# Expert 2's rows gathered inside expert 0's further tiles, and weights issued ahead of the turning of tiles 4 and 5

## The chip, the cores and the metric

The kernel runs on one core of a Trainium2 chip. A core has five engines with a queue each: TensorE (PE, matmuls), VectorE (DVE), ScalarE (ACT), GpSimd (POOL) and SyncE (SP), which here only issues transfers. Each queue works in order; the engines wait for each other through semaphores. Transfers issued by SP and POOL run on the core's 16 DMA engines. The metric is the device time of one execution in microseconds (us); lower is better.

## What is computed

A banded attention (8 batches, 8 heads, 576 positions, 64 per head) and behind it a mixture of 8 experts, top 1, on its 4608 rows of 512 numbers. Cut to what matters here:

```
logits = x @ w_gate;  e_idx = argmax(logits)
for e in range(8):
    mask = e_idx == e
    h = relu(x[mask] @ w1[e])                       # 512 -> 1024
    out[mask] = gate_w[mask] * eom[mask, e] * (h @ w2[e])   # 1024 -> 512
```

x is the attention's output. All is float32 at the interface. Which rows belong to an expert is known only when the gate of the last rows has been computed.

## The kernel before

The first 185 us or so are the attention, the gate and the ranking that gives every token a place in its expert's list (`src` holds the row numbers). Then the experts follow one after another, and the change lies there.

Each expert has up to SLOTS = 6 tiles of 128 rows. Tiles 0 to 3 (BASE = 4) always run; tiles 4 and 5 run as far as the expert has rows, through a `tc.Switch` with five bodies at the end of each expert's pass (L1346), the first of which (`nothing`) runs no further tile. Expert 0 is special: its first three tiles (HEAD = 3) run while the last rows are still being ranked (`head`, with `during_first` and `during_second`), and its next two in `two_more(0, HEAD, xx, next_x)`. Behind these stands a Switch for rare cases (L1284), whose second body (`repair`) computes expert 0's first tiles again where a late row displaced an early one.

A matrix product in float32 is made of three products of parts: each operand is split into a rounded part and a remainder. The names that the profile shows:

- `wraw`: four staging buffers of 512 KB in which `load_w(e, kind)` puts a quarter each of an expert's first (kind 0) or second matrix, four DMAs on SP (L114). `split_w` makes the two parts: ACT rounds (L132), DVE subtracts (L136). The subtract frees the staging buffer for the next load.
- `xg[0]` to `xg[3]` (the profile calls them sd) and `xg[4]`, `xg[5]` (xg): tiles of rows. `gather_rows(e, ...)` fetches an expert's rows into them with one indirect DMA for each tile, on POOL (L152).
- `turn_rows(e, ...)` brings a tile's rows into the order in which a 32 by 32 transpose on DVE completes the turn: SP writes the tile to the DRAM buffer `xq` in blocks (L170) and reads it back (L175), and the read waits for the landing of the write.
- `prep4`: the transpose on DVE (L190), the rounding on ACT (L197), the subtract on DVE (L198). Tiles 0 to 3 become `X` (sc in the profile), tiles 4 and 5 `xx` (xxh, xxl).
- `base_h` and `products1` (L210): the products with the first matrix, 12 matmuls for each of the NF = 8 blocks of 128 columns of h, into the accumulators `ph` (tpx). `relu` (L216 on ACT, L217 on DVE) makes the two parts of h.
- `gemm2` (L946): the products with the second matrix; `finish` scales (L953, L955), and `scatter` (L959, POOL) writes rows to the output.

The order on every engine is written out by hand: the whole section stands in `tc.manual_schedule` for all five engines, so each queue holds its instructions in the order of the program. In the pass of expert e the first products' blocks 2 to 7 carry the splits of its own second matrix (blocks 2 to 5), the gathers and the turning; the second products carry the splits of the next expert's first matrix and, after each, the `prep4` of one of its tiles, then `prep4` of tiles 4 and 5, then the gathers for expert e + 2. Blocks 0 and 1 of the next expert (`start(e + 1)`, and `fill` or a body's own calls) are queued on the TensorE around the Switch.

So for SP the order in the pass of an expert e above 1 is: turning of expert e + 1's four tiles (at the third block), turning of tiles 4 and 5 of expert e (at the sixth block), the four loads of expert e + 1's first matrix, the four of its second. For e = 1 the gathers of expert 2 stand at the third block behind those of tiles 4 and 5, and the turning of expert 2's rows stands at the sixth block, behind that of tiles 4 and 5 and ahead of the loads.

Of the kernel before, what the change touches and what calls it, by code (L numbers as in the profile page):

```python
# [31 lines left out]
BASE = 4  # L32
# [4 lines left out]
HEAD = 3  # L37
# [13 lines left out]
def kernel(  # L51
# [58 lines left out]
    def load_w(e, kind):  # L110
        src = (w1, w2)[kind]
        for c in range(4):
            t = stage.tile([P, 1024], F32, name="wraw")
            nc.sync.dma_start(out=t, in_=src[e, :, 1024 * c : 1024 * c + 1024])  # L114
            raws[e, kind, c] = t
# [22 lines left out]
    def split_w(e, kind, c, sub=nc.vector):  # L138
        split_hi(e, kind, c)
        split_lo(e, kind, c, sub)  # L140

    def part_of(w, a, o, n):
        return w[a][o // 1024][:, o % 1024 : o % 1024 + n]
# [3 lines left out]
    def where(e, j):  # L147
        s = e * SLOTS + j
        return idx[:, s : s + 1], scl[:, s : s + 1]

    def gather(j, at, rows=N):
        nc.gpsimd.indirect_dma_start(  # L152
            out=xg[j],
            out_offset=None,
            in_=xs[0:rows],
            in_offset=bass.IndirectOffsetOnAxis(ap=at.bitcast(U32), axis=0),
            bounds_check=rows - 1,
            oob_is_err=False,
        )

    def gather_rows(e, *js):
        if e < E:
            for j in js:
                gather(j, src[:, e * SLOTS + j : e * SLOTS + j + 1])

    def turn_rows(e, *js):
        if e < E:
            rows = {j: xq[P * (e * SLOTS + j) : P * (e * SLOTS + j) + P] for j in js}
            for j in js:
                nc.sync.dma_start(  # L170
                    out=rows[j].rearrange("(q s) (a f) -> (s a) q f", q=4, a=4),
                    in_=xg[j].rearrange("p (q f) -> p q f", q=4),
                )
            for j in js:
                nc.sync.dma_start(out=xg[j], in_=rows[j])  # L175

    def bank(ps, name):
        return ps.tile([P, 512], F32, name=name)

    def prep(j, xh, xl, k, tp):  # L180
        for c in range(NC):
            nc.tensor.transpose(out=tp[:, P * c : P * c + P], in_=xg[j][:, P * c : P * c + P], identity=idn)
        r = slice(P * k, P * k + P)
        tv = tp.rearrange("p (c t) -> p c t", c=NC)
        nc.scalar.copy(out=xh[:, :, r], in_=tv)
        nc.vector.tensor_tensor(out=xl[:, :, r], in0=tv, in1=xh[:, :, r], op=ALU.subtract)

    def prep4(j, xh, xl, k):
        t = xg[j]
        nc.vector.transpose(out=t, in_=t)  # L190
        r = slice(P * k, P * k + P)

        def view(ap):
            return ap.rearrange("p c (a s) -> p c a s", a=4)

        tv = t.rearrange("p (a c s) -> p c a s", a=4, c=NC)
        nc.scalar.copy(out=view(xh[:, :, r]), in_=tv)  # L197
        nc.vector.tensor_tensor(out=view(xl[:, :, r]), in0=tv, in1=view(xh[:, :, r]), op=ALU.subtract)  # L198
# [5 lines left out]
    def products1(e, fc, xh, xl, m, ph, chunks=range(NC), parts=(0, 1)):  # L204
        w = W[e, 0]
        for c in chunks:
            o = F * c + P * fc
            for a, x in ((0, xh), (0, xl), (1, xh)):
                if a in parts:
                    nc.tensor.matmul(  # L210
                        ph[:, 0:m], lhsT=part_of(w, a, o, P), rhs=x[:, c, 0:m],
                        start=c == 0 and x is xh and a == 0, stop=c == NC - 1 and a == 1,
                    )
# [8 lines left out]
    def base_h(e, fc, X, m, hs=None, ph=None):  # L222
        hh, hl = hs or hb[fc]
        return gemm1(e, fc, *X, m, ph or bank(ps_h, "ph"), hh[:, 0:m], hl[:, 0:m])
# [750 lines left out]
    def pair_x():  # L975
        return [mp.tile([P, NC, 2 * P], F32R, name=n) for n in ("xxh", "xxl")]
# [5 lines left out]
    def start(e):  # L982
        base_h(e, 0, X, BASE * P)
        return bank(ps_h, "ph")

    def go_on(ph):
        return [hb[0], relu(BASE * P, ph, *hb[1])]
# [57 lines left out]
    def choose(e):  # L1045
        flag[e] = nc.values_load(cnt[0:1, 2 * E + 3 + e : 2 * E + 4 + e], min_val=0, max_val=len(PATHS))
        flag[e, "hint"] = tc.switch_hint({t: flag[e] for t in HINTED}, len(PATHS) + 1, f"paths{e}")
# [77 lines left out]
    def two_more(e, j, xx, between=None):  # L1125
        h = []
        for fc in range(NF):
            if fc % 2 == 0:
                eh = ep.tile([P, 512], F32R, name=f"eh{fc // 2}")
                el = ep.tile([P, 512], F32R, name=f"el{fc // 2}")  # L1130
            r = slice(2 * P * (fc % 2), 2 * P * (fc % 2) + 2 * P)
            h.append(gemm1(e, fc, *xx, 2 * P, bank(ps_x, "tpx"), eh[:, r], el[:, r]))
        if between:
            between()
        for k in range(2):
            y = bank(ps_y, "y")
            for fc in range(NF):
                gemm2(e, fc, h[fc], k, y)
            finish(k == 0, *where(e, j + k), y)
# [117 lines left out]
    def next_x():  # L1257
        for j in range(BASE):
            prep4(j, *X, j)

    two_more(0, HEAD, xx, next_x)
    ph = start(1)
# [2 lines left out]
    def repair():  # L1265
        with tc.If(flag[0] > (HEAD + 2) * P):
            late = pair_x()
            prep(SLOTS - 1, *late, 0, bank(ps_x, "tpx"))
            extra(0, SLOTS - 1, late, 1, 0)
        with tc.If(flag["redo"] > 0):  # L1270
            places = [where(0, j) for j in range(HEAD)]
            for j in range(HEAD):
                gather(j, places[j][0])
            for j in range(HEAD):
                prep(j, *X, j, bank(ps_x, "tpx"))
            head(X, places, bank(ps_z, "z"), alone=True)
            gather_rows(1, *range(HEAD))
            turn_rows(1, *range(HEAD))
            for j in range(HEAD):
                prep4(j, *X, j)  # L1280
            base_h(1, 0, X, BASE * P)
            products1(1, 1, *X, BASE * P, ph)

    for n in tc.Switch(flag["rare"], 2, flag["rare", "hint"]):  # L1284
        products1(1, 1, *X, BASE * P, ph, (1, 2, 3))
# [3 lines left out]
    for e in range(1, E):  # L1289
        xx = pair_x()  # L1290
        h = go_on(ph)
        for fc in range(2, NF):
            h.append(base_h(e, fc, X, BASE * P, ph=bank(ps_x, "tpx") if fc % 4 > 1 else None))
            if fc == 2:
                gather_rows(e, 4, 5)
                if e > 1:
                    turn_rows(e + 1, *range(BASE))
                else:
                    gather_rows(2, *range(BASE))
            if fc < 6:  # L1300
                split_w(e, 1, fc - 2)
                if fc == 5:
                    turn_rows(e, 4, 5)
                    if e == 1:
                        turn_rows(2, *range(BASE))
                    if e + 1 < E:
                        load_w(e + 1, 0)
        choose(e)
        ys = [bank(ps_y, "y"), bank(ps_z, "z"), bank(ps_y, "y"), bank(ps_z, "z")]
        for fc in range(NF):  # L1310
            for j in range(BASE):
                gemm2(e, fc, h[fc], j, ys[j])
            if e + 1 < E and fc < 4:
                split_w(e + 1, 0, fc)
                if fc == 3:
                    load_w(e + 1, 1)
                prep4(fc, *X, fc)
            if fc in (4, 5):
                prep4(fc, *xx, fc - 4)
            if fc == 5:  # L1320
                if e > 2:
                    nc.gpsimd.drain()
                gather_rows(e + 2, *range(BASE))
        for j in range(BASE):
            finish(j % 2, *where(e, j), ys[j])
        fill = ()
        if e + 1 < E:
            ph = start(e + 1)
            fill = [lambda cs=cs: products1(e + 1, 1, *X, BASE * P, ph, cs) for cs in ((0,), (1,), (2, 3))]

        def nothing():
            for f in fill:
                f()

        def two():
            nothing()
            two_more(e, BASE, xx)

        bodies = [
            nothing,  # L1340
            lambda: extra(e, BASE, xx, 0, 1, fill),
            lambda: extra(e, BASE, xx, 1, 0, fill),
            lambda: extra(e, BASE, xx, 1, 1, fill),
            two,
        ]
        for n in tc.Switch(flag[e], len(bodies), flag[e, "hint"]):  # L1346
            bodies[n]()
# [165 lines left out]
```

## Time and profile before

| what | us |
|---|---|
| median of 3 runs (613.67 to 616.11) | 614.93 |
| the profiled execution | 612.23 |
| its span, first to last instruction | 610.5 |
| TensorE busy in the span | 579.5 (95%) |
| DVE, ACT, POOL busy | 351.8, 259.7, 219.3 |
| mean granted TensorE clock | 0.989 of full |

In the profile "idle before" and the brackets at the end of a line name the time an engine stood still ahead of an instruction and what let it go; "issue" means that it waited for nothing that the profile shows. PEld is the TensorE's load of weights into the array; a "q" behind an engine's name (SPq, POOLq, PEldq) marks work of its queue that is not counted as busy, such as issuing a DMA, a branch or a wait. "In order of time" is the view that lists the instructions of a stretch with their start and length; times count from the start of the span. In this run expert 1 takes its Switch's first body, as do experts 3 and 5.

### The profile page before, as it was taken

To read this page: it belongs to the slowest core of one execution; us is meant where nothing else is said; L and a number is where in the kernel's file an instruction comes from. 1 tells how busy PE (TensorE), PEld (TensorE's weight loads), DVE (VectorE), ACT (ScalarE), POOL (GpSimd) and SP (SyncE) were. 2 spreads that over 40 slices of the span, in tenths; PEclk is the share of its full clock that TensorE was granted. 3 is DMA by queue.
4 is the path that set the end of the run, shared out by engine and by line. 5 is a ranking of instruction groups with operands and counts; after the bars stand their busy time and mean duration, and the time that the engine had idled before them with its cause. 6 is when DMAs were issued, how large, how long until landed. Compare 5 with 4: busy or idle time off the path is not lost. (4 is left out here: it accounts for less than half of the span.)

```text
span 610.5 us, 13435 instructions
## 1 busy us (share of the span) xinstructions
PE 579.5 (95%) x5102; PEld 467.7 (77%) x5103; DVE 351.8 (58%) x621; ACT 259.7 (43%) x418; POOL 219.3 (36%) x364
## 2 busy tenths in 40 slices
PE   7799999998999999979999998999999999999995
PEld 6677777776787988868888887887588778758884
DVE  5888988899699335175561563563256456435020
ACT  4579665678443224144341442442244244233020
POOL 7788778788117214024131113013121310211021
PEclk8999999999999999989999999999999999999998
DMA  7998989896525914867756467747145764303021
GB/s 206 344 337 272 320 295 298 238 333 184 201 80 166 300 53 146 278 201 224 246 189 201 161 216 251 231 157 225 43 148 198 247 229 139 114 11 100 3 72 37
DMA packets 67509, 117.42 MB, mean 192 GB/s; under 512 B 7776, under 2 KB 44128, under 8 KB 65776
## 3 DMA queue, kind: packets, MB, share of 16 engines
q1 hardware_dynamic: 59904, 95.45, 47.9%
q0 software_dynamic: 6944, 19.15, 10.2%
q8 instruction: 67, 1.10, 0.8%
q14 instruction: 130, 1.06, 0.6%
q10 hardware_dynamic: 464, 0.66, 0.3%
HBM read 88.48 MB, written 30.28 MB: 195 GB/s over the span
## 5 line engine op out<-in xcount | busy, mean ns | idle before, releaser
L959 POOL DMA_INDIRECT out_dram<-yt,idx x39 | 38.6, 991 | 136.8 <-ACT yt L955 79.9
L152 POOL DMA_INDIRECT sd<-xs,src x28 | 29.4, 1048 | 122.7 <-DVE sc L198 120.5
L210 PE MATMUL ph<-sc,w 128*128 128x512 f32 x240 | 60.5, 405 | 3.2 <-ACT sc L197 3.2
L136 DVE TENSOR_TENSOR w<-wraw,w 128x1024 fp32r<-128x1024 f32 x40 | 49.2, 1233 | 18.1 <-ACT w L132 18.1
L210 PE MATMUL tpx<-sc,w 128*128 128x512 f32 x240 | 56.3, 390 | 2.9 <-issue 1.9
L210 PEld LDWEIGHTS ph<-sc,w 128*128 128x128 f32 x240 | 46.4, 195 | 15.4 <-ACT sc L197 3.7
L210 PEld LDWEIGHTS tpx<-sc,w 128*128 128x128 f32 x240 | 44.8, 188 | 13.2 <-issue 2.8
L946 PE MATMUL y<-w,h 128*128 128x512 f32 x190 | 53.9, 391 | 1.0 <-DVE w L136 1.0
L386 POOL TENSOR_TENSOR half<-half 128x128 f32<-128x128 f32 (+3 forms) x136 | 45.3, 333 | 10.7
L132 ACT CAST w<-wraw 128x1024 fp32r<-128x1024 f32 x40 | 41.6, 1044 | 10.4 <-DMA wraw<-in_w_dram 9.9
L946 PE MATMUL z<-w,h 128*128 128x512 f32 x152 | 43.5, 389 | 0.0
L946 PEld LDWEIGHTS y<-w,h 128*128 128x128 f32 x190 | 35.4, 188 | 8.6 <-issue 1.4
L197 ACT CAST sc<-sd 128x512 fp32r<-128x512 f32 x28 | 17.4, 621 | 53.1 <-DVE sd L190 53.1
L380 POOL TENSOR_TENSOR half<-pt 128x256 f32<-128x256 f32 x34 | 30.0, 882 | 11.3 <-ACT pt L375 9.9
L217 DVE SCALAR_TENSOR_TENSOR h<-tpx,h 128x512 fp32r<-128x512 f32 x28 | 19.4, 691 | 24.8 <-ACT h L216 24.7
L955 ACT ACTIVATE yt<-y,scl 128x512 f32<-128x512 f32 x19 | 12.9, 688 | 47.8 <-PE y L946 47.6
L946 PEld LDWEIGHTS z<-w,h 128*128 128x128 f32 x152 | 28.5, 188 | 5.9
L216 ACT ACTIVATE h<-tpx 128x512 fp32r<-128x512 f32 x28 | 16.8, 599 | 38.0 <-PE tpx L210 35.6
L198 DVE TENSOR_TENSOR sc<-sd,sc 128x512 fp32r<-128x512 f32 x28 | 19.4, 692 | 20.5 <-ACT sc L197 20.5
L375 ACT ACTIVATE pt<-pt 128x512 f32<-128x512 f32 x36 | 22.7, 632 | 18.8 <-DVE pt L365 14.6
L152 POOL DMA_INDIRECT xg<-xs,src x14 | 17.2, 1231 | 36.2 <-DMA sd<-xq 9.6
L361 DVE TENSOR_REDUCE mx<-sp 128x8 f32<-128x512 f32 x36 | 24.7, 685 | 8.5 <-PE sp L346 8.3
(296 smaller groups left out, 1393.9 us busy)
## 6 DMA issues: line engine op xcount, KB each, us to landing
wraw<-in_w_dram SPq DMA_DIRECT2D x64, 512.0 KB, 4.0
xq<-sd SPq DMA_DIRECT2D x28, 256.0 KB, 4.8
sd<-xq SPq DMA_DIRECT2D x28, 256.0 KB, 5.3
xs<-wraw SPq DMA_DIRECT2D x29, 128.0 KB, 5.7
xq<-xg SPq DMA_DIRECT2D x14, 256.0 KB, 2.3
xg<-xq SPq DMA_DIRECT2D x14, 256.0 KB, 2.7
sd<-in_qT_dram SPq DMA_DIRECT2D x6, 576.0 KB, 5.5
sa<-in_kT_dram SPq DMA_DIRECT2D x6, 576.0 KB, 6.8
```

The lines of the kernel that those rows point to most:

```text
L132: nc.scalar.copy(out=W[e, kind][0][c], in_=raws[e, kind, c])
L136: sub.tensor_tensor(out=w[1][c], in0=raws.pop((e, kind, c)), in1=w[0][c], op=ALU.subtract)
L152: nc.gpsimd.indirect_dma_start(out=xg[j], out_offset=None, in_=xs[0:rows], in_offset=bass.IndirectOffsetOnAxis(ap=at.bitcast(U32), axis=0) ...
L198: nc.vector.tensor_tensor(out=view(xl[:, :, r]), in0=tv, in1=view(xh[:, :, r]), op=ALU.subtract)
L210: nc.tensor.matmul(ph[:, 0:m], lhsT=part_of(w, a, o, P), rhs=x[:, c, 0:m], start=c == 0 and x is xh and a == 0, stop=c == NC - 1 and a == 1,)
L217: nc.vector.scalar_tensor_tensor(out=hl, in0=ph[:, 0:m], scalar=0.0, in1=hh, op0=ALU.max, op1=ALU.subtract)
L361: nc.vector.tensor_reduce(out=mx, in_=sp.rearrange("p (h k) -> p h k", h=H), axis=AX.X, op=ALU.max)
L375: nc.scalar.activation(out=pt, in_=pt, func=AF.Exp, scale=1.0 / 8.0)
L380: nc.gpsimd.tensor_tensor(out=half.rearrange("p (h c) k -> p h c k", c=2), in0=pv[:, :, :, 0:32], in1=pv[:, :, :, 32:64], op=ALU.add)
L386: nc.gpsimd.tensor_tensor(out=dst, in0=half[:, :, 0:n], in1=half[:, :, n : 2 * n], op=ALU.add)
L946: nc.tensor.matmul(y, lhsT=l[:, r], rhs=part_of(w, a, DM * fc, DM), start=fc == 0 and n == 0, stop=fc == NF - 1 and n == 2)
L959: put = nc.gpsimd.indirect_dma_start(out=out, out_offset=bass.IndirectOffsetOnAxis(ap=at.bitcast(U32), axis=0), in_=yt, in_offset=None, bo ...
```

## The change

The gathers of expert 2's four tiles, and of tile 4 of expert 1, move from the third block of expert 1 into `next_x`, which `two_more` calls for expert 0 between the first and the second products, right behind the `prep4` of expert 1's tiles. `repair` fetches again what it overwrites. The turning of expert 2's rows moves to the third block of expert 1, where the other experts have theirs. In all experts the loads of the next expert's first matrix are issued ahead of the turning of tiles 4 and 5, on SP.

```
@@ -1257,6 +1257,8 @@
     def next_x():
         for j in range(BASE):
             prep4(j, *X, j)
+        gather_rows(2, *range(BASE))
+        gather_rows(1, 4)
...
@@ -1280,6 +1282,8 @@
             products1(1, 1, *X, BASE * P, ph)
+        gather_rows(2, *range(HEAD))
+        gather_rows(1, 4)
...
@@ -1292,19 +1296,14 @@
             if fc == 2:
-                gather_rows(e, 4, 5)
-                if e > 1:
-                    turn_rows(e + 1, *range(BASE))
-                else:
-                    gather_rows(2, *range(BASE))
+                gather_rows(e, *((4, 5) if e > 1 else (5,)))
+                turn_rows(e + 1, *range(BASE))
             if fc < 6:
                 split_w(e, 1, fc - 2)
                 if fc == 5:
-                    turn_rows(e, 4, 5)
-                    if e == 1:
-                        turn_rows(2, *range(BASE))
                     if e + 1 < E:
                         load_w(e + 1, 0)
+                    turn_rows(e, 4, 5)
```

## Prediction

> **What bounds the kernel now.** I read the page first (the busy shares, the slices and the costliest groups), then the table of waits of the TensorE, then the order in time of each engine around the one long wait in the stretch that the change touches, and last the TensorE's branches.
>
> ```profile
> PE 579.5 (95%) x5102; PEld 467.7 (77%) x5103; DVE 351.8 (58%) x621; ACT 259.7 (43%) x418; POOL 219.3 (36%) x364
> ```
>
> The TensorE is busy for 579.5 of 610.5 us, so this change can only be worth the TensorE's idle time that it takes away, and the time at a low clock behind it. The table of waits of the TensorE from 190 us on (engine and line, who let it go, sum, times, longest) says how much there is:
>
> ```profile
> PE tpx L210 <- issue: 3.4, 2, 1.9
> PE ph L210 <- ACT sc L197: 3.2, 1, 3.2
> ```
>
> One wait of 3.2 us stands out: block 0 of expert 2 waits for the rows of expert 2 (sc) to be split. In order of time on the TensorE, with the same pair of blocks of a later expert for comparison, and the granted clock of the slow stretch (columns: stretch, length, PE, PEld, DVE, ACT, POOL busy, clock, DMA share, GB/s):
>
> ```profile
> 266.03 0.84 PE L946 MATMUL z<-sb,h 128*128 128x512 f32 x3
> 270.12 8.52 PE L210 MATMUL ph<-sc,w 128*128 128x512 f32 x24 [3.24 <-ACT sc L197]
> ...
> 372.27 5.60 PE L210 MATMUL ph<-sc,w 128*128 128x512 f32 x24
> 270.10:278.40 8.30, 8.28 (x24) 6.30 (x25) 5.33 (x8) 3.01 (x5) 3.86 (x4) 0.66 0.70 224
> ```
>
> The gap is 3.24 us, and the 24 matmuls behind it take 8.52 us at a mean clock of 0.66 where the same 24 take 5.60 us elsewhere. The bubble costs 3.24 + 2.92 = 6.16 us. Its cause stands in the order of time of ACT, DVE and SP in expert 1:
>
> ```profile
> 255.73 1.05 ACT L132 CAST w<-wraw 128x1024 fp32r<-128x1024 f32 x1 [9.93 <-DMA wraw<-in_w_dram]
> 270.10 0.69 DVE L198 TENSOR_TENSOR sc<-sd,sc 128x512 fp32r<-128x512 f32 x1 [0.69 <-ACT sc L197]
> 234.97 2.06 SPq L170 DMA_DIRECT2D xq<-xg  x2
> ...
> 240.59 4.91 SPq L170 DMA_DIRECT2D xq<-sd  x4
> ...
> 248.66 13.32 SPq L114 DMA_DIRECT2D wraw<-in_w_dram  x6
> ```
>
> SP is a queue in order. It issues the turning of tiles 4 and 5 (xg), then that of expert 2's rows (sd), and only at 248.66 the weights of expert 2. ACT waits 9.93 us for the first of these, and the chain split, turn, split behind it ends with the subtract at 270.10, 3.4 us after the TensorE is through with expert 1 (266.03 + 0.68 = 266.71).
>
> **The change part by part.** *Four gathers of expert 2 and one of tile 4, on POOL inside expert 0's further tiles.* Each sd is free when its last subtract is done, and POOL is idle there but for the scatters of expert 0:
>
> ```profile
> 220.22 0.69 DVE L198 TENSOR_TENSOR sc<-sd,sc 128x512 fp32r<-128x512 f32 x1 [0.69 <-ACT sc L197]
> 221.85 0.98 POOL L959 DMA_INDIRECT out_dram<-yt,idx  x1 [17.33 <-DVE yt L953]
> 232.65 1.04 POOL L152 DMA_INDIRECT xg<-xs,src  x1 [7.67 <-ACT h L216]
> L1284 POOLq INC_SWDGE_SEM  x1: 520/520/520, 228.1 to 228.1; - x1
> 214.93 0.32 SPq L175 DMA_DIRECT2D sd<-xq  x1
> ```
>
> The fourth gather is free at 220.91 and tile 4's follows; at 1.0 us and 0.3 us between them they end at 223.5, so the scatters go out up to 2 us later than now. Nobody computes on a scatter; what is queued behind them is POOL's own passage of the rare branch, where it lets its outstanding transfers land and bumps their semaphore at 228.1. I put that near 230 after the change, and tile 5's gather stays near 233. DVE and ACT get no instruction more. Cost on the path: nothing, covered by POOL's idle 17.33 us.
>
> *Turning of expert 2's rows at the third block.* SP can take it as soon as POOL has passed the branch, about 230; it took 8.1 us before (240.59 to 248.66), so it ends near 238. Early bound: 219, if only the landings hold it (SP leaves its last turn at 214.93); late bound: 234.97, SP's first issue now, and then 243.
>
> *Weights of expert 2 ahead of the turning of tiles 4 and 5.* A load needs its staging buffer, which the splits of expert 1's second matrix free on DVE; and it needs its time to land:
>
> ```profile
> 241.33 1.23 DVE L136 TENSOR_TENSOR sb<-wraw,sb 128x1024 fp32r<-128x1024 f32 x1 [0.24 <-ACT sb L132]
> DMA to landing us min/median/max: 3.5/3.9/10.6
> ```
>
> The four go out between 238 and 242.6 instead of 248.66 to 250. The first lands near 242, at worst near 248.6; ACT has been free for it since 255.73 − 9.93 = 245.80. The 9.93 us of waiting goes (at worst 2.8 of it stays), and the whole chain moves up by as much: its last subtract starts at 260.17 and ends 5.85 us before 266.71. That margin swallows even the worst landing. The gap goes, and the low clock with it: −6.16 us.
>
> *Turning of tiles 4 and 5 behind the weights.* In expert 1 SP reaches it at about 243 (the last load at 242.6). The two pairs took from 234.97 to 240.59, so the rows are there by about 252 with a landing; they are used at 270.70 − 9.93 = 260.77. In the later experts the turning waits for the fourth split as well:
>
> ```profile
> 270.70 0.70 DVE L190 STREAM_TRANSPOSE xg<-xg 128x512 f32<-128x512 f32 x1
> 290.35 1.81 SPq L170 DMA_DIRECT2D xq<-xg  x2
> 291.18 1.22 DVE L136 TENSOR_TENSOR w<-wraw,w 128x1024 fp32r<-128x1024 f32 x1 [0.24 <-ACT w L132]
> 298.68 1.05 ACT L132 CAST sa<-wraw 128x1024 fp32r<-128x1024 f32 x1 [3.02 <-DMA wraw<-in_w_dram]
> 313.70 0.70 DVE L190 STREAM_TRANSPOSE xg<-xg 128x512 f32<-128x512 f32 x1
> ```
>
> In expert 2 it moves from 290.35 to about 292.8, and its rows are wanted at 313.70, or 3.02 us sooner since that wait of ACT goes too: some 10 us to spare. These 3.02 us buy nothing, for the TensorE does not wait there. Experts 3 to 6 have the same order with no wait of either kind: nothing.
>
> *What is late next.* Behind block 0 and 1 of the next expert stands a branch of several ways, and the TensorE takes it while it works off 24 queued matmuls (5.45 us, from 1.4 us after the first). The branch's duration in ns and its start (the rare branch, expert 1's, expert 3's), the DMA share of the stretches of the last two, the TensorE's two gaps by issue, behind the branches of experts 3 and 5, and SP's last load and first turning around the branches of experts 3 and 1:
>
> ```profile
> L1509 PEldq COMPARE_BRANCH  x1: 4175/4175/4175, 224.2 to 224.2; - x1
> L1509 PEldq COMPARE_BRANCH  x1: 3327/3327/3327, 273.2 to 273.2; - x1
> L1509 PEldq COMPARE_BRANCH  x1: 5972/5972/5972, 373.7 to 373.7; - x1
> 272.00:277.00 5.00, 5.00 (x16) 3.90 (x15) 3.73 (x6) 2.45 (x5) 1.82 (x3) 0.63 0.56 161
> 373.00:381.00 8.00, 6.08 (x27) 4.76 (x26) 0.92 (x2) 0.60 (x1) 2.84 (x4) 1.00 0.94 310
> 379.79 1.38 PE L210 MATMUL tpx<-sc,w 128*128 128x512 f32 x5 [1.92 <-issue]
> 489.49 1.63 PE L210 MATMUL tpx<-sc,sa 128*128 128x512 f32 x6 [1.51 <-issue]
> 369.73 2.31 SPq L170 DMA_DIRECT2D xq<-sd  x4
> 268.82 0.33 SPq L114 DMA_DIRECT2D wraw<-in_w_dram  x1
> 274.19 1.38 SPq L170 DMA_DIRECT2D xq<-sd  x2
> ```
>
> With the DMA engines at 0.94 the branch took 5.97 us, 1.9 us more than the queued matmuls cover; at 0.56 it took 3.33 us. In expert 3 SP turned the next rows at 369.73, 2.5 us before block 0 at 372.27. In expert 1 now it does so at 274.19, 4.1 us after block 0 at 270.12, so its branch was quick. With the chain 9.93 us sooner, the last load leaves at about 258.9 and the turning, 5.37 us behind it as now, at 264.3 or sooner: 2.4 us before block 0 at 266.71. Expert 1 gets the timing of expert 3, and I take the mean of the two such gaps, 1.92 and 1.51: +1.72 us. The ends are 0 (the quick branch) and 1.92. No clock is lost with it: around the 1.92 us gap the clock stayed at 1.00 (the stretch from 373 to 381).
>
> Two other branches come nearer to traffic. The rare one at 224.2 ends 0.1 us after its cover; the five gathers and later scatters add to a stretch in which few transfers run. The nearest row is itself: 0, with −0.1 (3.33 us) and +1.8 us (5.97 us) as ends. Expert 2's turning comes 3.02 us earlier, to about its block 0; in expert 4 it stood there too (next fence) and no gap followed: 0, at most +2.
>
> ```profile
> 417.96 2.88 PE L210 MATMUL ph<-sc,w 128*128 128x512 f32 x12
> 418.14 2.66 SPq L170 DMA_DIRECT2D xq<-sd  x4
> ```
>
> The sum: −3.24 − 2.92 + 1.72 = −4.44 us. The profiled execution took 612.23 us (span 610.5, 1.7 outside it), so it becomes 607.8; its runs' median is 2.7 us higher, 614.93, and becomes 610.5 us.
>
> **The rivals.** *The next branch stays quick.* If SP's turning of expert 2 starts only at 234.97, the chain moves up by 5 us rather than 9.93, the rows of expert 3 are turned after the branch has its code, as now, and the gap is still gone. 614.93 − 6.16 = 608.8. For it: two quick branches of 3.33 and 4.18 us; against it: the two with a turning just ahead of the block were followed by the gaps.
>
> *One more branch is hit.* If SP is not held by POOL's passage, it turns expert 2's rows from about 219 on, and the rare branch at 224.2 runs into that traffic: 5.97 us, +1.8 us, 612.3. The same price, about, if it is expert 2's branch. For it: the gathers land by then; against it: POOL holds its semaphores until 228.1 now. The Trainium skill, "Runtime: NRT & Kernel Launch", Instruction fetch mechanics, speaks for this rival: a taken branch out of the loaded window waits for a DMA to bring the code. The trace agrees, with 5.97 us at a DMA share of 0.94 against 3.33 us at 0.56.
>
> *It does not do what it says.* The turning of expert 2's rows, still ahead of the weights on SP, begins, for a wait that I do not see, no sooner than at 240.59; the weights then go out at 248.66 and all stays: 614.9. Against it: the two pairs of xg no longer stand before it.
>
> *The low clock has another cause.* Then the 3.24 us of gap go and the 2.92 us stay: 614.93 − 3.24 + 1.72 = 613.4. Against it: of the two pairs of blocks above only the one behind the long gap ran at 0.66. The Trainium skill, "TensorE: Matmul & The Clock Gate", Part 1, would give this result, for it halves the clock after an idle window of about 3.4 us, which a gap of 3.24 us need not fill. The trace differs, with 0.66 right behind that gap.
>
> *Slower.* The rows of tile 5 come late: their transpose on DVE stands ahead of expert 1's result scaling and of block 0's relu of expert 2. Lateness up to 266.71 is covered by the 5.85 us of margin; 6.16 − 1.72 = 4.4 us more eat the gain, so from a landing at about 271 on (if the TensorE has to follow at once) the kernel loses. At 275 it would be 618.9. Against it: about 252 by the rows, 19 us earlier.
>
> **How the numbers follow.** Forecast 0.52, quick branch 0.20, one more branch 0.18, no effect 0.04, clock 0.02, slower 0.04. 0.5% is about what a measurement of this kernel can tell from no change; 3.07 us of gain is reached by the forecast (4.4; I leave 0.02 of it below) and by the quick branch: faster 0.70. Same: 0.02 + 0.18 + 0.04 + 0.02 = 0.26. Slower: 0.04. The forecast's own range is 609.3 to 611.7 (the runs now lie 1.2 us to each side). With the quick branch at 608.8 less part of that spread and the extra branch at 612.3 plus it: 608.0 to 613.4.
>
> **What would show it.** Right: ACT no longer waits for wraw before L132 in experts 1 and 2; the TensorE has no gap before expert 2's block 0 and clock 1.00 there; a new gap by issue of 1.5 to 1.9 us some 5.5 us behind that block's start, with a branch of 5.5 to 6 us; SP turns expert 3's rows 2.5 us before the block. Wrong: a branch of under 4.1 us there (608.8); a gap behind the rare branch (612.3); ACT still waiting for weights, or DVE for tile 5.

## The result, and the profile after

| | before | after |
|---|---|---|
| median of 20 runs each (us) | 613.78 (609.36 to 620.12) | 608.26 (603.7 to 615.17) |
| ratio | | 0.9903 (95%: 0.9877 to 0.993) |
| the profiled execution | 612.23 | 605.33 |
| its span | 610.5 | 603.5 |
| mean granted clock in it | 0.989 | 0.997 |

The kernel is faster by about 1%, 5.5 us by the medians and 6.9 us between the two profiled executions, where 4.44 us were forecast; the ratio leaves disturbed runs out, so it is not quite that of the medians. 20 runs put the time before at 613.78, 1.15 us under the median of three that the forecast was set against.

The busy line of the page and the TensorE's waits from 190 us on, of the kernel after:

```profile
PE 573.1 (95%) x5076; PEld 465.4 (77%) x5103; DVE 349.7 (58%) x621; ACT 259.5 (43%) x418; POOL 220.2 (36%) x364
...
PE tpx L210 <- PE ph L210: 1.7, 2, 0.9
PE tpx L210 <- issue: 1.2, 1, 1.2
```

The wait for sc, 3.2 us before, is gone. What is left are three small gaps of the blocks behind a branch (tpx), put down here to the matmul before them or to nothing. In order of time on the TensorE around expert 2's block 0 and around the gaps behind the branches of experts 3 and 5, with the three branches (ns, and where they start) and the clock and DMA share of the first:

```profile
266.15 5.60 PE L210 MATMUL ph<-sc,w 128*128 128x512 f32 x24
...
272.68 5.71 PE L210 MATMUL tpx<-sc,w 128*128 128x512 f32 x24 [0.93 <-PE ph L210]
372.68 5.70 PE L210 MATMUL tpx<-sc,w 128*128 128x512 f32 x24 [0.79 <-PE ph L210]
482.44 1.61 PE L210 MATMUL tpx<-sc,sa 128*128 128x512 f32 x6 [1.20 <-issue]
L1508 PEldq COMPARE_BRANCH  x1: 4977/4977/4977, 267.5 to 267.5; - x1
L1508 PEldq COMPARE_BRANCH  x2: 304/2572/4840, 365.3 to 367.7; - x2
L1508 PEldq COMPARE_BRANCH  x2: 308/2780/5252, 474.6 to 477.0; - x2
266.10:272.70 6.60, 5.67 (x26) 4.38 (x25) 1.44 (x2) 0.86 (x2) 3.16 (x4) 1.00 1.02 294
```

Block 0 follows expert 1's last matmul without a gap (265.47 + 0.68 = 266.15) at a clock of 1.00. The new gap that the prediction put behind expert 1's branch is there, 0.93 us where 1.72 was forecast, with the DMA engines at 1.02. Expert 3's shrank from 1.92 to 0.79 and expert 5's from 1.51 to 1.20, which nothing in the prediction said.

SP's queue and ACT's start of the splits in expert 1, in order of time:

```profile
229.11 2.66 SPq L170 DMA_DIRECT2D xq<-sd  x4
232.00 4.33 SPq L175 DMA_DIRECT2D sd<-xq  x4
236.38 5.97 SPq L114 DMA_DIRECT2D wraw<-in_w_dram  x4
242.46 0.93 SPq L170 DMA_DIRECT2D xq<-xg  x2
246.84 1.12 SPq L175 DMA_DIRECT2D xg<-xq  x2
...
259.11 0.33 SPq L114 DMA_DIRECT2D wraw<-in_w_dram  x1
264.94 3.95 SPq L170 DMA_DIRECT2D xq<-sd  x4
...
246.09 1.05 ACT L132 CAST w<-wraw 128x1024 fp32r<-128x1024 f32 x1 [0.85 <-issue]
260.39 0.69 DVE L198 TENSOR_TENSOR sc<-sd,sc 128x512 fp32r<-128x512 f32 x1 [0.69 <-ACT sc L197]
```

Expert 2's rows are turned from 229.11 (230 forecast), its weights leave from 236.38 (238) to 242.35 (242.6), tiles 4 and 5 follow at 242.46 (243), and the last subtract starts at 260.39 (260.17). Only the last step is off: SP turns expert 3's rows at 264.94, 1.2 us ahead of block 0 and not 2.4. Two things make up the difference: ACT began its splits 0.85 us after it was free, and SP took 5.83 us from its last load (259.11) to this turning, where the prediction had 5.37.

### The profile page after: what moved, and what is told of

It is laid out like the page before. It is cut to its first block, busy times and chain, and to the rows that moved or that the text cites. A ratio compares the mean times of both kernels' runs of the same rounds, so it can differ in the third digit from the quotient of the medians.

```text
span 603.5 us, 13393 instructions
## 1 busy us (share of the span) xinstructions
PE 573.1 (95%) x5076; PEld 465.4 (77%) x5103; DVE 349.7 (58%) x621; ACT 259.5 (43%) x418; POOL 220.2 (36%) x364
## 5 line engine op out<-in xcount | busy, mean ns | idle before, releaser
L210 PE MATMUL ph<-sc,w 128*128 128x512 f32 x240 | 57.6, 391 | 0.0
L210 PEld LDWEIGHTS ph<-sc,w 128*128 128x128 f32 x240 | 44.7, 188 | 10.7 <-issue 1.7
```

What stands on the lines that cost most here:

```text
L210: nc.tensor.matmul(ph[:, 0:m], lhsT=part_of(w, a, o, P), rhs=x[:, c, 0:m], start=c == 0 and x is xh and a == 0, stop=c == NC - 1 and a == 1,)
```

## The experiments

Each ratio is to the kernel before on the same chip, in brackets its 95% interval. Kernels of one group of four shared a chip.

**The early gathers and turning alone.** The weights stay behind the turning of tiles 4 and 5:

```
-                    if e + 1 < E:
-                        load_w(e + 1, 0)
                     turn_rows(e, 4, 5)
+                    if e + 1 < E:
+                        load_w(e + 1, 0)
```

> Gathers early and expert 2's rows turned at the third block, as in the change, but the turning of tiles 4 and 5 stays ahead of the weights on SP. Theory (what held expert 2's weights up was the turning of expert 2's rows standing late, not the turning of tiles 4 and 5): that turning ends near 236, tile 5's gather has landed near 237, the two pairs take 5 us, the weights leave at about 242 to 243 and land near 247; ACT waits under 2 us for wraw in expert 1, the TensorE has no gap before expert 2's block 0, and the time is that of the changed kernel within 1 us (about 5.5 us under before). Rival (the order on SP is what counts): the weights leave near 247, ACT waits 5 us or more, and a gap of 1 us or more is left before block 0; at most half of the gain.

607.62 us, 0.9897 (0.9846 to 0.9949). SP and ACT of this kernel in expert 1, expert 2's block 0, the second of the two blocks around the branch of expert 3, and that branch:

```profile
239.80 1.08 SPq L175 DMA_DIRECT2D xg<-xq  x2
240.99 8.71 SPq L114 DMA_DIRECT2D wraw<-in_w_dram  x5
ACT w L132 <- DMA wraw<-in_w_dram: 1.7, 1, 1.7
266.21 5.60 PE L210 MATMUL ph<-sc,w 128*128 128x512 f32 x24
373.53 7.32 PE L210 MATMUL tpx<-sc,w 128*128 128x512 f32 x24 [2.15 <-issue]
L1508 PEldq COMPARE_BRANCH  x1: 6196/6196/6196, 367.2 to 367.2; - x1
```

The theory holds for the bubble: the weights leave at 240.99, ACT waits 1.7 us, and no gap is left before block 0. So it was the late gathering and turning of expert 2's rows that held the weights up; the order of the loads is not needed for that. But the gaps behind the branches of experts 3 and 5 are 2.15 and 1.98 us, that behind expert 1's is 0.31, and behind the 2.15 us the matmuls ran slow, 7.32 us for 24. By its span, 605.9, this kernel is 3.9 us over the changed kernel beside it (602.0); so "within 1 us" is missed by the medians too (607.62 and 605.2), though the intervals of the two overlap.

**The order of the loads alone.** The gathers of before, and `load_w(e + 1, 0)` ahead of `turn_rows(e, 4, 5)` and `turn_rows(2, ...)`:

```
                 if fc == 5:
+                    if e + 1 < E:
+                        load_w(e + 1, 0)
                     turn_rows(e, 4, 5)
                     if e == 1:
                         turn_rows(2, *range(BASE))
-                    if e + 1 < E:
-                        load_w(e + 1, 0)
```

> The weights go ahead of the turning of tiles 4 and 5 and of expert 2's rows on SP, but the gathers and the turning of expert 2's rows stay where they were. Theory (expert 2's rows must be there early too): ACT no longer waits for wraw, but expert 2's rows are turned only from about 247 on and land near 256, so the first transpose of sd waits until then, the chain ends about 1 us sooner than before, and a gap of about 2 us or more is left before expert 2's block 0; 0 to 3 us under before, depending on whether the clock falls behind the shorter gap. Rival (the weights alone were late): no gap, 5.5 us under before.

609.39 us, 0.9934 (0.99 to 0.9969). DVE and SP in expert 1, and the TensorE at expert 2's block 0:

```profile
257.12 0.71 DVE L190 STREAM_TRANSPOSE sd<-sd 128x512 f32<-128x512 f32 x1 [7.67 <-DMA sd<-xq]
250.13 2.77 SPq L170 DMA_DIRECT2D xq<-sd  x4
269.29 0.50 PE L210 MATMUL ph<-sc,w 128*128 128x512 f32 x1 [1.81 <-ACT sc L197]
270.02 7.12 PE L210 MATMUL ph<-sc,w 128*128 128x512 f32 x23 [0.22 <-DVE sc L198]
```

Now DVE waits for rows in place of ACT for weights, and 2.03 us of gap stay, with 7.12 us for 23 matmuls behind them. Rows and weights both have to be early, and the first is the one that brings the second. By the medians it is 3.4 us under before, a little more than the 0 to 3 expected; the gaps of experts 3 and 5 are 1.26 and 0.85 us here, 1.3 us less in all than in the first profile of the kernel before.

**The changed kernel again.**

> The changed kernel as it is, on the chip of the other three. If the small gaps behind the branches of experts 1, 3 and 5 (0.93, 0.79 and 1.20 us) come from transfers in the way of the code, each is between 0.5 and 2 us again; if the drop of expert 3's gap from 1.92 to 0.79 came from the new order, it stays under 1.2. Time: about 5.5 us under before.

605.2 us, 0.9894 (0.9845 to 0.9944). The blocks behind the branches of experts 1, 3 and 5:

```profile
271.02 2.29 PE L210 MATMUL tpx<-sc,w 128*128 128x512 f32 x9 [0.76 <-PE ph L210]
371.43 5.73 PE L210 MATMUL tpx<-sc,w 128*128 128x512 f32 x24 [1.22 <-issue]
481.14 1.63 PE L210 MATMUL tpx<-sc,sa 128*128 128x512 f32 x6 [1.35 <-issue]
```

The gaps are 0.76, 1.22 and 1.35 us. They are there again; expert 3's at 1.22 doesn't tell between the two readings.

**The turning later.** In every expert SP turns the next expert's rows behind the first quarter of the next weights (`load_w` takes the quarters to load as a new third argument; its own lines are left out here):

```
             if fc == 2:
                 gather_rows(e, *((4, 5) if e > 1 else (5,)))
-                turn_rows(e + 1, *range(BASE))
             if fc < 6:
                 split_w(e, 1, fc - 2)
+                if fc == 2 and e + 1 < E:
+                    load_w(e + 1, 0, (0,))
+                    turn_rows(e + 1, *range(BASE))
                 if fc == 5:
                     if e + 1 < E:
-                        load_w(e + 1, 0)
+                        load_w(e + 1, 0, (1, 2, 3))
```

> As the changed kernel, but in every expert SP turns the next expert's rows behind the first quarter of the next weights, which waits for a split of the third block, so some 14 us after the next expert's block 0 and not 2.4 us ahead of it. Theory (the turning's transfers keep the TensorE's branch from its code): the branches of experts 1, 3 and 5 take 3.3 to 4.2 us in place of 4.8 to 5.3, the three gaps of 0.8 to 1.2 us go, and the time is 2 to 3 us under the changed kernel. Rival (the branch takes that long whatever runs beside it, or the four scatters suffice): gaps of 0.8 us or more stay and the time is that of the changed kernel.

603.06 us, 0.9851 (0.9802 to 0.99). Its branches of experts 1, 3 and 5, the two blocks around the first, and the stretch around each with clock and DMA share; the last line is the first of these stretches in the changed kernel:

```profile
L1510 PEldq COMPARE_BRANCH  x1: 3877/3877/3877, 266.9 to 266.9; - x1
L1510 PEldq COMPARE_BRANCH  x1: 3817/3817/3817, 365.9 to 365.9; - x1
L1510 PEldq COMPARE_BRANCH  x1: 3832/3832/3832, 474.3 to 474.3; - x1
265.52 5.60 PE L210 MATMUL ph<-sc,w 128*128 128x512 f32 x24
270.96 2.30 PE L210 MATMUL tpx<-sc,w 128*128 128x512 f32 x9
264.00:273.00 9.00, 9.00 (x41) 7.30 (x40) 2.19 (x3) 2.18 (x4) 4.40 (x5) 1.00 0.37 128
363.00:372.00 9.00, 9.00 (x41) 7.34 (x40) 2.25 (x4) 2.23 (x4) 5.03 (x5) 1.00 0.37 128
471.00:480.00 9.00, 9.00 (x41) 7.32 (x41) 2.84 (x4) 2.23 (x4) 4.25 (x5) 1.00 0.36 123
...
264.00:273.00 9.00, 8.07 (x37) 6.39 (x36) 2.79 (x4) 2.29 (x4) 3.98 (x4) 1.00 0.82 239
```

With the DMA engines at 0.37 in place of 0.82 over these nine us (0.58 in place of 1.00 over expert 1's branch alone) all three branches take under 3.9 us and the three gaps are gone; the scatters stood where they stood. The span, 599.4, is 2.6 us under the changed kernel's beside it, the median 2.1 us; the intervals of the two overlap. The turning's transfers made the branches slow. The profile's list of DMA packets shows where the time goes: inside each of these branches one packet of 16 KB of the kind "instruction" runs. At expert 1 it starts 2.6 us after the branch in the changed kernel and 1.5 us with the later turning (3.0 and 1.0 us in the slow and the quick branch of experts 3 and 1 before), and the branch ends 2.3 to 2.9 us behind that start in all four. So what the turning delays is the start of this packet. Run again among the next four, it gave 603.14 us, 0.9859 (0.981 to 0.9908), with one gap of 0.25 us:

> The kernel with the later turning again, beside the others: no gap behind any of the branches of experts 1, 3 and 5, and about 9 us under before (0.985); if the first reading was chance, a gap of 0.8 us or more and the changed kernel's 0.990.

**A faster chain.** This tests why the gaps of experts 3 and 5 shrank. Ahead of ACT's first split stands `choose(e)`, a register load that tells the engine its body. The instruction's duration in ns, of the kernel after in expert 1 and of the kernel before in expert 3, and ahead of the latter, in the kernel before, SP's loads and the DMA share:

```profile
L1046 ACTq TENSOR_LOAD <-cnt x1: 982/982/982, 244.7 to 244.7; - x1
L1046 ACTq TENSOR_LOAD <-cnt x1: 283/283/283, 350.8 to 350.8; - x1
346.17 2.31 SPq L114 DMA_DIRECT2D wraw<-in_w_dram  x4
349.50:351.10 1.60, 1.60 (x9) 1.33 (x8) 0.00 (x0) 0.33 (x1) 0.00 (x0) 1.00 1.00 379
```

In the kernel after it is 0.7 us slower, the splits start as much later, and the turning with them. The expectation below puts this down to the weights in flight, and that can't be all: in the kernel before, weights were in flight too, with the DMA engines at 1.00, and the load took 0.28 us. What the loads ahead of the turning changed is that the turning of tiles 4 and 5 (SP, 242.46) now runs during the register load. In the changed kernel's two profiles it takes 0.59 to 1.13 us in experts 1 to 6; in the three with the loads behind the turning 0.28 to 0.30 us, but for one of 0.88 us in expert 1, where expert 2's rows were being turned. That the turning is the cause is likely and not shown: with the later turning two loads took 0.43 and 0.59 us. In the experiment the choice is read at the third block, on every engine:

```
             if fc == 2:
+                choose(e)
                 gather_rows(e, *((4, 5) if e > 1 else (5,)))
...
-        choose(e)
```

> As the changed kernel, but each expert's choice of its body (a register load on every engine, which stood ahead of ACT's first split of the next weights and took 0.95 us there in place of 0.28, with the weights in flight) is read at the third block. Theory (the smaller gaps behind the branches come from that later start, which moves the turning 0.7 us back towards the branch's end): ACT's split starts 0.7 us sooner, SP turns 2.4 us or more ahead of block 0 in experts 3 and 5, their branches take 5.5 us or more and the gaps grow from about 1.1 to 1.5 to 2.1 us; expert 1's gap grows by as much. So a chain that is faster makes the kernel 1 to 3 us slower than the changed one. Rival (the gaps vary by chance, or depend on the order of the loads by itself): gaps of 0.8 to 1.4 us as now, and no change.

609.84 us, 0.9941 (0.9903 to 0.9978), where the changed kernel gave 0.9903 and 0.9894. ACT's split follows its relu at once, and around the branches of expert 1 (turning, branch, blocks) and of experts 3 and 5 it looks like this:

```profile
247.22 1.04 ACT L132 CAST w<-wraw 128x1024 fp32r<-128x1024 f32 x1
266.57 2.41 SPq L170 DMA_DIRECT2D xq<-sd  x4
L1508 PEldq COMPARE_BRANCH  x2: 317/3117/5917, 267.2 to 269.6; - x2
268.24 5.60 PE L210 MATMUL ph<-sc,w 128*128 128x512 f32 x24
275.71 7.31 PE L210 MATMUL tpx<-sc,w 128*128 128x512 f32 x24 [1.87 <-issue]
378.38 5.72 PE L210 MATMUL tpx<-sc,w 128*128 128x512 f32 x24 [1.57 <-issue]
488.08 1.62 PE L210 MATMUL tpx<-sc,sa 128*128 128x512 f32 x6 [1.48 <-issue]
275.70:283.00 7.30, 7.29 (x25) 5.88 (x26) 2.18 (x3) 2.25 (x3) 2.06 (x2) 0.77 0.38 127
```

The gaps grow to 1.87, 1.57 and 1.48 us, and the first one costs clock besides (0.77, 7.31 us for 24 matmuls). The turning stands 1.7 us ahead of expert 1's block 0, less than the 2.4 us that the theory gave for experts 3 and 5 (there it is 2.1 and 2.2); the edit puts SP's own register load right ahead of the turning, and from its start to the turning 0.64 us pass (265.93 to 266.57). The direction holds: all three gaps are above all six of the changed kernel's two profiles (0.76 to 1.35 us). But the lead of the turning does not settle the gap alone: 1.7 us of it go with a gap of 1.87 here, and 1.9 us with one of 0.79 in the changed kernel's expert 3. That the kernel is slower for it, by 0.4 to 0.5% in the middle of the ratios, the times alone don't show, for the intervals overlap; the gaps in the trace say where it would come from. With the later turning the same edit costs nothing, as it should:

> The kernel with the later turning, and with the choice read at the third block too. Theory: the turning starts after the branch in any case, so the 0.7 us sooner start of the chain changes nothing: branches of experts 1, 3 and 5 of 3.3 to 4.2 us, no gap, the time of the kernel with the later turning within 1 us. Rival (reading the choice early costs or gains by itself): 1 us or more to either side.

602.63 us, 0.9844 (0.9795 to 0.9894), no gap over 0.26 us behind these branches: the time of the kernel with the later turning. The three runs with the later turning lie at 0.9844 to 0.9859 and the two of the changed kernel at 0.9894 and 0.9903, so this version is the faster one by each of these ratios, if not clear of their intervals.

**The kernel before again.**

> The kernel before, looked at once more. Theory: the bubble ahead of expert 2's block 0 is there again (3 us or more, and half the clock behind it), and the gaps of experts 3 and 5 are 1.5 us or more again, with the turning about 2.5 us ahead of the block. Rival (the gaps vary by chance): one of them at 1.2 us or less.

One time of 613.86 us. The TensorE at expert 2's block 0 and behind the branches of experts 3 and 5:

```profile
271.68 8.69 PE L210 MATMUL ph<-sc,w 128*128 128x512 f32 x24 [3.10 <-ACT sc L197]
381.24 2.09 PE L210 MATMUL tpx<-sc,w 128*128 128x512 f32 x8 [1.55 <-issue]
490.92 1.62 PE L210 MATMUL tpx<-sc,sa 128*128 128x512 f32 x6 [1.23 <-issue]
```

The bubble is the same, 3.10 us and 8.69 us. Expert 5's gap of 1.23 us misses the expectation of 1.5 or more: with the same order the gap varies by some tenths.

## Why the prediction came out as it did

The time, 608.26 us, lies 1.0 us below the forecast's own range (609.3 to 611.7) and just inside the wide one that takes in the rivals (608.0 to 613.4). Part of that is the start: from the 20 runs' 613.78 us the sum of −4.44 gives 609.34. The rest is a drop larger than the sum, by 1.1 us between the medians and 2.5 us between the two profiles. That 608.26 lies near the 608.8 of the rival with a quick next branch is chance: that branch took 4.98 us and left a gap. By its steps:

- **The bubble (−6.16 us): right, term by term.** The 3.24 us are gone, and the 24 matmuls take 5.60 us again. The chain of causes was right, with one shift that the runs brought out: the change's own order of the loads is not what removes the bubble; the early gathers and turning do.
- **Costed at nothing: right.** POOL's gathers and later scatters, the rare branch (no gap behind it), tiles 4 and 5 later (their rows are used at 261.00; SP read them back from 246.84 on, and they landed 2.8 us after each issue, some ten microseconds before) and expert 2's branch (none).
- **The step that failed is "what is late next".** Its mechanism was right, its size was not: +1.72 us forecast, +0.93 and +0.76 measured. I shifted the whole chain by ACT's 9.93 us of waiting and overlooked that the new order puts the turning of tiles 4 and 5 beside the register load ahead of the split, which takes 0.98 in place of 0.29 us there; SP's way from its last load to the turning, 5.83 us, was 0.46 us longer than the 5.37 that I carried over. The turning came 1.2 us ahead of block 0 rather than 2.4, and the branch was through sooner, after 4.98 us rather than 5.5 to 6.
- **"Experts 3 to 6: nothing" failed, likely for the same reason.** I gave it for the waits that these experts don't have, but the new order of the loads holds for them too: the same register load takes 0.95 and 1.05 us in experts 3 and 5 after and 0.28 us before, and SP turns 1.9 and 1.6 us ahead of block 0 in place of 2.5. In the profiles with the loads behind the turning, or with the choice read early, the gaps of experts 3 and 5 are 1.92, 1.51, 2.15, 1.98, 1.57, 1.48, 1.55 and 1.23 us, mean 1.67; with the loads ahead and the choice in its place 0.79, 1.20, 1.22, 1.35, 1.26 and 0.85, mean 1.11. That is about −0.6 us for each of the two, and −1.13 and −0.31 us between the two profiles compared here, where chance has its part. Between the two profiles, −6.16 + 0.93 − 1.13 − 0.31 = −6.67 of the −6.9 us are named.
- **Of the rivals** none came out. The one of a low clock with another cause falls: the low clock goes with the gap, and in three experiments it followed a gap again. My "no clock lost" behind a gap of up to 2 us held for the changed kernel and not in general.

Left open is what the rest of the scatter of the gaps comes from (1.23 to 1.92 us with one and the same kernel), what slows the register load, and whether it is the number of the turning's packets or their bytes that holds up the branch's own packet; none of these was tried apart.

## What to carry to other kernels

When a queue in order feeds an engine, look for what stands ahead of the late transfer, and then for why that was late itself: here the weights waited behind a turning, and the turning behind gathers that could go out 20 us sooner (214.73 in place of 235.59). Treat the branch of a busy engine as one more reader of the DMA engines, and keep bursts such as the turning's out of the few microseconds ahead of it. A chain that gets faster only moves its transfers; ask what they meet where they land, for moving the same burst some 13 us back was worth nearly half as much again as the change (2.1 to 2.6 us beside 5.5, by the middle values).

## What the hardware showed that I had not expected

- The TensorE's branches of experts 1, 3 and 5 took 3.3 to 4.3 us where SP's turning started after the block, 4.4 us where it started 0.5 us ahead of it, and 4.8 to 6.2 us where it started 1.1 to 2.7 us ahead. The 24 queued matmuls hide 4.05 us: each of the gaps is the branch's duration less that. In the slow branches a 16 KB instruction packet among the DMA packets starts later, 2.6 to 3.0 us after the branch in place of 1.0 to 1.5 in the four compared above.
- A register load on ACT took 0.28 us beside weight loads that kept the DMA engines at 1.00, and 0.59 to 1.13 us while tiles 4 and 5 were being turned.
- The clock halved for a short time behind gaps of 1.87 us (0.50 from 276.7 to 280.0 us, 0.77 over 7.3 us), 2.03 and 2.15 us, while gaps of 1.92 and 1.98 us cost none. I can give no threshold from this.
